# Queries of one batch item transposed by DMA instead of TensorE, with the loads behind them held and reordered

## The chip, the cores and the metric

One core of a Trainium2 chip runs the whole kernel. The metric is the device time of one execution in microseconds; a median of several runs is given. Before the change it is 173.47 us (172.95 to 173.8, 4 runs). A kernel counts as faster or slower when it differs by more than 2%.

## The reference, cut to what matters

Four batch items with 8 heads, 768 positions and head width 64 pass through block-sorted attention, and the result through a small MLP.

```python
P = sinkhorn(sort_net)                           # 5 rounds, 8x8 blocks per head
k_sorted = einsum('bhij,bhjcd->bhicd', P, k_b)   # also for v
scores = scale * matmul(q_b, k_sorted^T)         # per block of 96 positions
attn = softmax(scores)
x = matmul(attn, v_sorted)                       # then heads side by side
out = maximum(x @ w1, x @ w2) @ w_out            # for every position
```

## The kernel before

The program is laid out by hand: each engine executes its own list in the order of the Python code. The MLP of item b runs beside the attention of item b+1, as "units" of matmuls with "steps" of attention between them. An eviction copies a result from PSUM, where matmuls write, to SBUF; a transfer lands when its data are in place. "Packing" sets the queries of two heads side by side, and "turning" copies reorder loaded values. The parts that matter here:

```python
def pair_q(b, two):            # VectorE (DVE) packs two heads' queries side by side
    nc.vector.tensor_copy(out=q_pair[b][...], in_=q_raw[b][...])

def q_transposes(b, half):
    if b > 1:                  # items 2 and 3: transposed by DMA, from the sync queue
        nc.sync.dma_start_transpose(out=qT[b][...], in_=q_pair[b][...])
        return
    ps = ps_bf16("tq_ps")      # items 0 and 1: on TensorE (PE); for item 1, 12 matmuls per half
    ...
    evac(qT[b][...], ps, ...)  # and an eviction from PSUM

def load_rest():               # called after an early unit of item 0
    load_q(1)
    load_k(2)
...
9: [pair_q(1, 0), pair_q(1, 1), load_v(2), load_v(3), load_q(2)],   # after unit 9
...
# the copies that turn the values of items 2 and 3 follow values steps of item 1:
tns = [lambda c=c: turn(both, c) for c in range(0, BLK, 12)]
VA[1:6] = [(lambda f=f, g=g: (f(), g())) for f, g in zip(VA[1:6], tns)]
TR[0:2] = [(lambda f=f, g=g: (f(), g())) for f, g in zip(TR[0:2], tns[5:])]
```

PSUM is one pool of four buffers (`psum = tc.tile_pool(name="psum", bufs=4, ...)`), and every matmul group needs one. Loads are issued by GpSimd (POOL), and cast float32 to bfloat16 on the way.

The softmax here doesn't subtract the row's maximum and nothing guards it: scores larger than these inputs give would overflow.

Of the kernel before, what the change touches and what calls it, by code (L numbers as in the profile page):

```python
# [9 lines left out]

FP32 = mybir.dt.float32
BF16 = mybir.dt.bfloat16
TWICE = 1


@with_exitstack
def kernel(
# [16 lines left out]
    nc = tc.nc  # L34
# [12 lines left out]
    R = S // 128  # L47
    PB = 128 // NB
    HP = H // 2
# [5 lines left out]
    const = ctx.enter_context(tc.tile_pool(name="const", bufs=1))  # L55
# [13 lines left out]
    def ps_bf16(name):  # L69
        return psum.tile([128, 2048], BF16, tag="ps", name=name)  # L70
# [28 lines left out]
    def evac(out_ap, in_ap, n, two_x=False, eng=None):  # L99
        a_ns, d_ns = (200 + n) / 1.2, (130 + (n / 2 if two_x else n)) / 0.96  # L100
        if eng:
            load[eng] += a_ns if eng == "A" else d_ns
        if (eng or pick(a_ns, d_ns)) == "A":
            nc.scalar.copy(out=out_ap, in_=in_ap)  # L104
        else:
            nc.vector.tensor_copy(out=out_ap, in_=in_ap)  # L106
# [5 lines left out]
    q_raw, qT = {}, {}  # L112
# [15 lines left out]
    def load_q(b):  # L128
        t = qpool.tile([128, H, R * D], BF16, tag="q_raw", name="q_raw", bufs=1)
        nc.gpsimd.dma_start(out=t, in_=q[b].rearrange("h (p r) d -> p h (r d)", r=R))  # L130
        q_raw[b] = t
# [9 lines left out]
    def load_k(b):  # L141
        k_raw[b] = kpool.tile([128, HB * D], BF16, tag="k_raw", name="k_raw")
        n = HB * D // NCH
        for ci in range(NCH):
            nc.gpsimd.dma_start(  # L145
                out=k_raw[b][:, ci * n : (ci + 1) * n],
                in_=k_src[b, :, ci * n : (ci + 1) * n],
            )

    def load_v(b, c0=0, pieces=2):  # L150
        r0 = (b % 2) * 64
        n = (BLK - c0) * D // pieces
        for m in range(pieces):
            nc.gpsimd.dma_start(
                out=v_raw[r0 : r0 + 64, c0 * D + m * n : c0 * D + (m + 1) * n],
                in_=v_src[b, :, c0 * D + m * n : c0 * D + (m + 1) * n],
            )
# [19 lines left out]
    ident = const.tile([128, 128], BF16, tag="ident", name="ident")  # L177
# [26 lines left out]
    def turn_v(rows, eng, c0, c1, d0=0, d1=D):  # L204
        dst = v_dc[rows, 0 : D * BLK].rearrange("p (d c) -> p d c", c=BLK)[:, d0:d1, c0:c1]
        src = v_raw[rows].rearrange("p (c d) -> p d c", d=D)[:, d0:d1, c0:c1]
        for _ in range(TWICE):
            if eng == "A":
                nc.scalar.copy(out=dst, in_=src)
            else:  # L210
                nc.vector.tensor_copy(out=dst, in_=src)  # L211


    rowsum = const.tile([G, NB], FP32, tag="rowsum", name="rowsum")
# [107 lines left out]
    q_pair = {}  # L322
# [11 lines left out]
    def q_transposes(b, half, eng=None):  # L334

        if half == 0:
            qT[b] = qpool.tile([128, HP, R, 128], BF16, tag="qT", name="qT")
        if b > 1:
            nc.sync.dma_start_transpose(
                out=qT[b][:, half * 2 : half * 2 + 2].rearrange("p h r c -> p (h r) c"),  # L340
                in_=q_pair[b][:, half * 2 : half * 2 + 2].rearrange("p h r e -> p (h r e)"),
            )
            return
        ps = ps_bf16("tq_ps")
        for m in range(2 * R):
            hp, r = half * 2 + m // R, m % R
            c = slice(m * 128, (m + 1) * 128)
            if b in q_pair:
                nc.tensor.matmul(  # L349
                    ps[:, c], q_pair[b][:, hp, r], ident, is_transpose=True, start=True, stop=True  # L350
                )
                continue
            for h2 in range(2):
                nc.tensor.matmul(  # L354
                    ps[h2 * 64 : h2 * 64 + 64, c],
                    q_raw[b][:, hp + 4 * h2, r * D : (r + 1) * D],
                    ident,
                    is_transpose=True,
                    start=True,
                    stop=True,  # L360
                )
        evac(
            qT[b][:, half * 2 : half * 2 + 2].rearrange("p h r c -> p (h r c)"),
            ps[:, 0 : 2 * R * 128],
            2 * R * 128,
            two_x=True,
            eng=eng,
        )
# [275 lines left out]
    def att(b):  # L644

        SC = [lambda u=u: scores(b, u) for u in range(8)]
        VA = [lambda u=u: values(b, u) for u in range(8)]
        TR = [lambda t=t: x_transposes(b, t) for t in range(4)]
        return SC, VA, TR
# [20 lines left out]
    SC, VA, TR = att(0)  # L670
# [33 lines left out]
    def turn(rows, c0):  # L704
        turn_v(rows, "D", c0, c0 + 12)
        load["D"] += 800

    def load_rest():
        load_q(1)
        load_k(2)  # L710

    tail = {
        0: [VA[4]],
# [13 lines left out]
        9: [  # L727
            lambda: pair_q(1, 0),
            lambda: pair_q(1, 1),
            lambda: load_v(2),  # L730
            lambda: load_v(3),
            lambda: load_q(2),
        ],
        22: [lambda: block_diagonals(2)],
        23: [lambda: block_diagonals(3)],
# [8 lines left out]
    for b in range(B):  # L744
        units = [lambda t=t: moe_h(b, 0, t, None if b else "A") for t in range(4)]
        if b == 0:
            units[0] = lambda: None
            units[1] = lambda: None
        wps = [lambda dmt=dmt: w_product(dmt, "A" if dmt == 1 else None) for dmt in range(4)]
        if b == 0:  # L750
            units += wps[:2]
        units += [lambda t=t: moe_h(b, 1, t) for t in range(4)]
        cost = [1.3] * 8
        if b == 0:
            units += wps[2:]
            cost[4:4] = [1.7] * 2
            cost += [1.7] * 2
        units += [
            lambda ti=ti, part=part: moe_out(b, ti, part)
            for ti in range(6 if b < B - 1 else 4)  # L760
            for part in range(2)
        ]
        cost += [1.3] * 12
        if b == B - 1:
            units += [
                lambda: moe_out_last(4, [(0, 512, "D")]),
                lambda: moe_out_last(5, [(0, 256, "A"), (256, 384, "D"), (384, 512, "A")]),
            ]
        steps, lo = [], 2
        if b < B - 1:  # L770
            qs = [lambda half=half: q_transposes(1, half) for half in range(2)]
            if b < 2:
                tail[18 - 4 * b] = [lambda two=two: pair_q(b + 2, two) for two in range(2)]
                tail[18 - 4 * b] += [lambda half=half: q_transposes(b + 2, half) for half in range(2)]
            ks = [lambda t=t, b=b: sort_k(b + 1, t) for t in range(3)]
            SC, VA, TR = att(b + 1)

            def group(*fs):
                return [lambda: [f() for f in fs]]

            if b == 0:
                lo = 10
                tail[9][2:2] = ks
                vs = [lambda t=t: sort_v(1, t) for t in range(4)]
                tns = [lambda c=c: turn(both, c) for c in range(0, BLK, 12)]
                VA[1:6] = [(lambda f=f, g=g: (f(), g())) for f, g in zip(VA[1:6], tns)]
                TR[0:2] = [(lambda f=f, g=g: (f(), g())) for f, g in zip(TR[0:2], tns[5:])]
                SC[7:] = [lambda f=SC[7], g=tns[7]: (f(), g())]
                steps = group(*vs[:3]) + qs[:1] + group(*SC[0:2], vs[3]) + qs[1:] + VA[:1]
                steps += group(*SC[2:5]) + VA[1:2]  # L790
            elif b == 1:
                vs = [lambda t=t: sort_v_pair(2, t) for t in range(8)]
                steps = group(*ks) + group(*SC[0:2], vs[0], late_loads)
                steps += group(*vs[1:4]) + group(*vs[4:7]) + group(*SC[2:4], vs[7]) + VA[:2]
            else:
                steps = group(*ks) + group(*SC[0:2])
                steps += VA[:1] + group(*SC[2:5]) + VA[1:2]
            rest = SC[4:] if b == 1 else SC[5:]
            steps[-1:] = group(VA[1], TR[0])
            steps += VA[2:3] + group(VA[3], TR[1])  # L800
            steps += group(*rest[:-1]) + VA[4:5] + rest[-1:] + group(VA[5], TR[2])
            steps += VA[6:7] + group(VA[7], TR[3])
        done = 0
        for n, unit in enumerate(units):
            unit()
            for step in tail.get(n, []):
                step()
            total = sum(cost[lo:-2])
            want = -(-len(steps) * sum(cost[lo : n + 1]) // total)
            while done < min(want, len(steps)):  # L810
                steps[done]()
                done += 1
        tail = {}
# [28 lines left out]
```

## Time and profile before

| | before |
|---|---|
| median time | 173.47 us |
| span of the profiled execution | 172.3 us |
| PE busy | 161.7 us, 94% |
| DVE busy | 88.4 us, 51% |
| item 1's MLP starts (PE) | 73.34 us |
| last loads of the first stage land | 58.9 us |

PE is the bound. The start of item 1's MLP is a good milestone: behind it both kernels do the same work on PE. Its line before the change:

```profile
73.34 4.07 PE L576 MATMUL h_ps<-xT,w_sb 128*128 128x384 bf16 x24
```

In the line of an instruction the columns are start, length, engine, source line, operation, output and input, count, and in brackets how long the engine was idle before it and what ended that.

### The profile page before, as it was taken

The page shows a single profiled execution, that of the slowest core. Times are in us where ns is not written, and L with a number is a line of the kernel's source. Part 1 is how long each engine was busy: PE and PEld are TensorE (multiplying, and loading weights), DVE is VectorE, ACT ScalarE, POOL GpSimd, SP SyncE. Part 2 cuts the span into 40 slices and gives each one's busy share as a digit, 9 for nine tenths or more (in the row PEclk, how much of TensorE's full clock was granted, in tenths as well). Part 3 has the DMA queues.
Part 4 walks back from the last instruction along what each step waited for, and adds up shares of the span by engine and source line. Part 5 has one row for each costly group of instructions (what it writes and reads, how often), then busy time and mean ns, then how long its engine had stood idle before and what let it go on. Part 6 is the DMA issues. An engine that isn't in the chain of part 4 may idle for free.

```text
span 172.3 us, 4531 instructions
## 1 busy us (share of the span) xinstructions
PE 161.7 (94%) x1997; PEld 98.1 (57%) x2015; DVE 88.4 (51%) x194; ACT 83.8 (49%) x101; POOL 24.5 (14%) x40
## 2 busy tenths in 40 slices
PE   7899999989999999998989899999999999999990
PEld 7847766735666555456655445575554546654470
DVE  5879677679656399810685255044452422320130
ACT  4599875864745554069971532465605404312000
POOL 7953362251300000000600000000000000000000
PEclk9999999999999999999999999999999999999998
DMA  3999999999999352993497549920035173000342
GB/s 49 201 206 207 199 207 210 207 205 207 220 212 199 60 167 51 166 233 122 58 203 117 101 135 203 182 109 4 0 51 147 37 198 125 0 0 0 122 183 65
DMA packets 29811, 23.11 MB, mean 134 GB/s; under 512 B 16672, under 2 KB 24736, under 8 KB 29792
## 3 DMA queue, kind: packets, MB, share of 16 engines
q0 software_dynamic: 10304, 12.58, 42.9%
q1 hardware_dynamic: 19200, 10.04, 23.2%
q8 instruction: 16, 0.26, 0.6%
q10 hardware_dynamic: 288, 0.20, 0.4%
q14 instruction: 3, 0.02, 0.0%
HBM read 25.17 MB, written 6.29 MB: 183 GB/s over the span
## 4 chain that ended last, share of the span: by engine, by line
PE 79%; DMA 7%; ACT 6%; POOL 2%; DVE 2%; issue 2%; ACTq 0%; POOLq 0%
PE out_ps L603 36%; PE h_ps L576 24%; DMA q_raw<-in_q_dram 7%; PE o_ps L473 5%; PE wc_ps L554 4%; PE s_ps L446 3%; PE k_ps L379 2%; ACT kT L104 2%; ACT g L590 1%; DVE g L592 1%; ACT w2T L104 1%; PE tw_ps L531 1%; PE tq_ps L349 1%; PE tq_ps L354 1%; POOL k_raw L145 1%
## 5 line engine op out<-in xcount | busy, mean ns | idle before, releaser
L603 PE MATMUL out_ps<-wo_sb,g 128*128 128x512 bf16 (+2 forms) x197 | 47.0, 362 | 1.1 <-ACT o L104 0.5
L576 PE MATMUL h_ps<-xT,w_sb 128*128 128x384 bf16 x256 | 44.8, 326 | 0.8 <-DVE g L592 0.6
L576 PEld LDWEIGHTS <-w_sb 128*128 128x128 bf16 x256 | 24.2, 97 | 16.3 <-issue 0.6
L454 ACT ACTIVATE e<-s_ps 96x768 bf16<-96x768 f32 x32 | 24.2, 807 | 15.8 <-PE s_ps L446 15.7
L603 PEld LDWEIGHTS <-g 128*128 128x128 bf16 x208 | 17.7, 97 | 15.9 <-issue 0.5
L590 ACT ACTIVATE g<-h_ps 128x768 bf16<-128x768 f32 x22 | 17.8, 813 | 16.4 <-PE h_ps L576 16.4
L104 ACT COPY o<-out_ps 128x1024 f32<-128x1024 f32 x10 | 10.1, 1012 | 31.4 <-PE out_ps L603 31.4
L603 PE MATMUL out_ps<-wc,xT 128*128 128x512 bf16 (+2 forms) x103 | 24.9, 362 | 0.1
L490 DVE TENSOR_TENSOR x<-o_ps,rs 96x512 bf16<-96x512 f32 x32 | 22.0, 687 | 1.1
L592 DVE TENSOR_SCALAR g<-h_ps 128x768 bf16<-128x768 f32 x10 | 9.6, 958 | 15.9 <-PE h_ps L576 15.6
L484 DVE RECIPROCAL rs<-o_ps 96x8 f32<-96x8 f32 x32 | 6.4, 201 | 21.7 <-PE o_ps L473 21.5
L603 PEld LDWEIGHTS <-xT 128*128 128x128 bf16 x104 | 9.9, 97 | 11.0
L211 DVE COPY v_dc<-v_raw 64x768 bf16<-64x768 bf16 (+2 forms) x18 | 15.5, 902 | 0.4 <-DMA v_raw<-in_v_dram 0.3
L473 PEld LDWEIGHTS <-e 96*128 96x128 bf16 x256 | 11.6, 97 | 6.6 <-DVE x L490 0.5
L106 DVE CAST v_sb<-v_ps 96x1024 bf16<-96x1024 f32 x7 | 8.5, 1215 | 11.8 <-PE v_ps L421 8.4
L473 PE MATMUL o_ps<-v_sb,e 96*128 96x65 bf16 x256 | 13.1, 193 | 0.1
L104 ACT CAST v_sb<-v_ps 96x1024 bf16<-96x1024 f32 x9 | 8.7, 1014 | 2.0 <-PE v_ps L400 1.9
L446 PEld LDWEIGHTS <-kT 64*128 64x128 bf16 x256 | 6.0, 94 | 6.2 <-issue 4.2
L446 PE MATMUL s_ps<-qT,kT 64*128 64x96 bf16 x256 | 8.7, 204 | 0.7 <-ACT kT L104 0.6
L104 ACT CAST kT<-k_ps 128x1024 bf16<-128x1024 f32 x9 | 8.6, 1021 | 0.7 <-PE k_ps L379 0.7
L82 PEld LDWEIGHTS <-fill 128*128 128x128 bf16 x109 | 7.6, 128 | 2.2 <-DVE fill L73 1.2
L554 PE MATMUL wc_ps<-wo_sb,w2T 128*128 128x512 bf16 x29 | 7.4, 380 | 0.7 <-ACT w2T L104 0.5
(76 smaller groups left out, 130.0 us busy)
## 6 DMA issues: line engine op xcount, KB each, us to landing
out_dram<-o SPq DMA_DIRECT2D x11, 512.0 KB, 3.0
k_raw<-in_k_dram POOLq DMA_DIRECT2D x12, 256.0 KB, 10.4
q_raw<-in_q_dram POOLq DMA_DIRECT2D x4, 768.0 KB, 12.6
v_raw<-in_v_dram POOLq DMA_DIRECT2D x6, 384.0 KB, 13.6
w_sb<-in_moe_w_dram POOLq DMA_DIRECT2D x3, 512.0 KB, 15.9
wo_sb<-in_moe_w_out_dram POOLq DMA_DIRECT2D x2, 512.0 KB, 19.4
v_raw<-in_v_dram POOLq DMA_DIRECT2D x3, 256.0 KB, 4.9
w_sb<-in_moe_w_dram POOLq DMA_DIRECT2D x2, 256.0 KB, 14.3
```

The costliest lines, as they stand in the source:

```text
L104: nc.scalar.copy(out=out_ap, in_=in_ap)
L106: nc.vector.tensor_copy(out=out_ap, in_=in_ap)
L211: nc.vector.tensor_copy(out=dst, in_=src)
L446: nc.tensor.matmul(ps[:, h2 * 512 + ii * 128 : h2 * 512 + ii * 128 + BLK], kT[b][rows, (hp * 8 + i) * BLK : (hp * 8 + i) * BLK + 128], rhs ...
L454: nc.scalar.activation(out=e[:, 0 : 8 * BLK].rearrange("p (t c r) -> p t c r", t=8, r=R), in_=ps[0:BLK].rearrange("p (t f) -> p t f", t=8) ...
L473: nc.tensor.matmul(ps[:, h2 * 512 + ii * 65 : h2 * 512 + (ii + 1) * 65], e[:, (h2 * 4 + ii) * BLK : (h2 * 4 + ii) * BLK + 128], v_sb[:, m0 ...
L490: nc.vector.tensor_tensor(out=x, in0=ov[:, :, :, 0:D], in1=rs.to_broadcast([BLK, 2, 4, D]), op=ALU.mult,)
L554: nc.tensor.matmul(wc_ps[0][:, m * 512 : (m + 1) * 512], w2T[:, fb, dmt * 128 : (dmt + 1) * 128], wo_sb[:, fb, :], start=(fb == 0), stop=( ...
L576: nc.tensor.matmul(h_ps[t][:, m * 512 : m * 512 + TCH], w1_sb[:, hp, fb * 128 : (fb + 1) * 128], xT[:, b % 2, ch, hp % 2, hp // 2, :], sta ...
L590: nc.scalar.activation(out=g, in_=src, func=AF.Relu)
L592: nc.vector.tensor_scalar(out=g, in0=src, scalar1=0.0, scalar2=None, op0=ALU.max)
L603: nc.tensor.matmul(dst, g_tiles[b, ch, m // 2][:, m % 2, off : off + 128] if m < NFB else xT[:, b % 2, ch, hp % 2, hp // 2, off : off + 12 ...
```

## The change

The intent: take the 24 transposes of item 1's queries off PE, the busy engine, by handing them to the DMA engines, as is done for items 2 and 3. While they run no load is to disturb them, so all later loads wait for them, by way of a one-element copy on GpSimd that reads the transposed result. Behind it the loads leave as values, keys, queries. (A loop over `TWICE = 1` and the branch for item 1's PE transposes also go, and the sorting of item 1's keys is put behind the new issues.)

```diff
-        if b > 1:
+        if b > 0:
             nc.sync.dma_start_transpose(
...
     def load_rest():
         load_q(1)
+
+    def middle_loads():
+
+        held = const.tile([1, 1], BF16, tag="held_m", name="held")
+        nc.gpsimd.tensor_copy(out=held, in_=qT[1][0:1, HP - 1, R - 1, 0:1])
+        load_v(2)
+        load_v(3)
         load_k(2)
+        load_q(2)
...
             lambda: pair_q(1, 0),
             lambda: pair_q(1, 1),
-            lambda: load_v(2),
-            lambda: load_v(3),
-            lambda: load_q(2),
+            lambda: q_transposes(1, 0),
+            lambda: q_transposes(1, 1),
+            middle_loads,
...
-                steps = group(*vs[:3]) + qs[:1] + group(*SC[0:2], vs[3]) + qs[1:] + VA[:1]
+                steps = group(*vs[:3]) + group(*SC[0:2], vs[3]) + VA[:1]
```

More of the change, by code (lines that the diff above doesn't have):

```diff
@@ L12 @@
 BF16 = mybir.dt.bfloat16
-TWICE = 1
 @with_exitstack
@@ L206, in turn_v @@
         src = v_raw[rows].rearrange("p (c d) -> p d c", d=D)[:, d0:d1, c0:c1]
-        for _ in range(TWICE):
-            if eng == "A":
-                nc.scalar.copy(out=dst, in_=src)
-            else:
-                nc.vector.tensor_copy(out=dst, in_=src)
+        if eng == "A":
+            nc.scalar.copy(out=dst, in_=src)
+        else:
+            nc.vector.tensor_copy(out=dst, in_=src)
     rowsum = const.tile([G, NB], FP32, tag="rowsum", name="rowsum")
@@ L347, in q_transposes @@
             c = slice(m * 128, (m + 1) * 128)
-            if b in q_pair:
-                nc.tensor.matmul(
-                    ps[:, c], q_pair[b][:, hp, r], ident, is_transpose=True, start=True, stop=True
-                )
-                continue
             for h2 in range(2):
@@ L770 @@
         if b < B - 1:
-            qs = [lambda half=half: q_transposes(1, half) for half in range(2)]
             if b < 2:
@@ L782 @@
                 lo = 10
-                tail[9][2:2] = ks
+                tail[9][4:4] = ks
                 vs = [lambda t=t: sort_v(1, t) for t in range(4)]
```

## The prediction

> **What bounds the kernel now.** I read the page first, then the chain of work that ended last, then the instructions of DVE, GpSimd's queue and the sync queue in order of time between 27 and 76 us, and the busy time in stretches of 4 us. The page says who is the bound, and how the transfers lie in time:
>
> ```profile
> PE 161.7 (94%) x1997; PEld 98.1 (57%) x2015; DVE 88.4 (51%) x194; ACT 83.8 (49%) x101; POOL 24.5 (14%) x40
> ...
> DMA  3999999999999352993497549920035173000342
> GB/s 49 201 206 207 199 207 210 207 205 207 220 212 199 60 167 51 166 233 122 58 203 117 101 135 203 182 109 4 0 51 147 37 198 125 0 0 0 122 183 65
> ```
>
> TensorE (PE) is at 94%, so the time falls only by what leaves PE or what it waits for, and every wait put into its path costs in full. The DMA row (slices of 4.3 us) is full from the start to about 56 us at a steady 205 GB/s: the loads run back to back.
>
> The stage that the change touches, item 1's attention beside item 0's MLP, in stretches (columns: stretch, length, busy us of each engine, clock, DMA share, GB/s):
>
> ```profile
> 44.00:48.00 4.00, 3.95 (x124) 2.83 (x125) 2.24 (x3) 2.63 (x3) 1.58 (x2) 1.00 1.12 219
> 48.00:52.00 4.00, 3.79 (x70) 2.67 (x68) 2.18 (x2) 2.19 (x3) 0.00 (x0) 1.00 1.03 213
> 52.00:56.00 4.00, 3.76 (x54) 2.59 (x50) 2.79 (x4) 2.17 (x3) 0.00 (x0) 1.00 1.18 197
> 56.00:60.00 4.00, 3.94 (x49) 2.08 (x49) 1.33 (x4) 2.20 (x3) 0.00 (x0) 1.00 0.41 64
> 60.00:64.00 4.00, 4.00 (x53) 2.23 (x53) 3.93 (x8) 2.52 (x3) 0.00 (x0) 1.00 0.62 180
> 64.00:68.00 4.00, 3.94 (x35) 1.88 (x33) 3.97 (x8) 1.68 (x2) 0.00 (x0) 1.00 0.26 51
> ```
>
> DVE (third busy column) is half idle until 60 us, and then full: 3.93 and 3.97 of 4.00 us. So here, against its 51% overall, DVE has no slack. What fills it, in order of time (start, length):
>
> ```profile
> 59.06 0.69 DVE L490 TENSOR_TENSOR x<-o_ps,rs 96x512 bf16<-96x512 f32 x1
> 59.66 1.57 DVE L211 COPY v_dc<-v_raw 128x768 bf16<-128x768 bf16 x2
> 61.15 0.21 DVE L484 RECIPROCAL rs<-o_ps 96x8 f32<-96x8 f32 x1
> ...
> 66.62 1.02 DVE L328 COPY q_pair<-q_raw 128x1536 bf16<-128x1536 bf16 x2
> ```
>
> The 59.66 copies turn the values of items 2 and 3; the 66.62 pair packs the queries of item 2. Both read what the loads bring, and neither waits today: the values' issues at 37.16 to 43.97 us land between 49.6 and 55.1 (12.4, 12.8, 14.0 and 11.1 us to landing), the queries issued at 45.31 land at 58.9.
>
> The chain over the removed work (start, us, what):
>
> ```profile
> 48.10 1.02 ACT v_sb L104
> 49.12 0.04 issue
> 49.16 0.83 PE tq_ps L349 x12
> ...
> 51.76 1.02 ACT wc L104
> 52.78 0.04 issue
> 52.82 0.83 PE tq_ps L349 x12
> ```
>
> Both groups of 12 transposes are on the path, each just after the eviction of an older PSUM buffer. That shows how the four buffers are handed out: the second group took the one that the wc eviction freed, although others had been given back; the oldest released in program order comes next. I use that below.
>
> **What the Trainium skill says.** "DMA: Bandwidth & Descriptors", section "Queues, rings and completion order": each DMA engine serves the queues it has work for in turn, by packet. So transposes from the sync queue and loads from GpSimd share the same engines: holding the loads keeps the transposes short, but later transposes and stores will slow the held loads. No row above measures that sharing alone. "VectorE: DVE Perf Modes", section "The three transpose paths": a DMA transpose is slower in itself than TensorE's (1309 against 390 ns for 128x128) but lands in SBUF without PSUM. Here the 12 on PE took 0.83 us, and a DMA one of the same half 3.8 to 4.4 us to landing. "PSUM — Partial Sum Buffer", section "Engine vs sequencer instructions": the queues of VectorE, ScalarE and GpSimd are strict FIFO. The trace agrees, as far as DVE's order above is the program's: a DVE copy that waits for a load holds up the evictions behind it.
>
> **The change, part by part.** Removed from PE: 24 transposes in two groups of 0.83 us, 1.66 us, all on the path. Also gone are about 0.35 us of PE waits for the buffers they needed. From DVE: two evictions of qT of 0.95 us, which ran while DVE had slack: worth nothing directly. Two PSUM turns fewer. The packing of item 1's queries (1.03 us of DVE from 43.99) stays.
>
> Added: two DMA transposes. The packing ends at 45.02, the sync queue is empty then (its first transpose today is at 59.77), so the first goes out at 45.1. From item 2's pair (67.73: the first instruction takes 2.58 us and lands after 4.4, the second lands after 3.8) and item 3's (101.57: 1.67 us, second lands after 4.2) the halves land at about 49.3 and 51.0 to 51.5. PE reaches the first scores at 49.1 to 49.2, as fewer steps stand before them: a wait of some 0.2 us. The half for heads 2 and 3 is wanted only after 53 us. Net so far: 1.66 + 0.35 - 0.2, about 1.8 us gained; I take 1.7. With nothing else, item 1's MLP (73.41 today) would start at 71.7.
>
> Moved: values 2 and 3, keys 2 and queries 2 leave after a GpSimd copy that reads qT. The same construction for item 3 took 0.5 us from the copy (82.46) to the first issue (82.95). So the first load goes out at about 51.7, instead of keys at 29.95 and values at 37.16. Queries 1 land at 44.0 as before (27.68 + 16.3), since they stood in front of the moved loads anyway. Hence the DMA engines, full today until about 57, do nothing but two transposes from 44 to about 53 us: 9 us of load time lost.
>
> When do values land? Keys and queries of item 3 are the same 1.57 MB from an empty queue: issued from 82.95, the last landed at 94.3 (84.53 + 9.8), 11.35 us. So the last piece of the values lands at 51.7 + 11.35 = 63.1, with some sharing with one transpose and one store 63.2 (my estimate). DVE wants it (its second turning copy, channels 60 to 71) at about 57.3, since the steps are now 13 instead of 15 and item 1's second values step comes one unit earlier than today. DVE stands still for nearly 6 us.
>
> What PE does meanwhile: it goes on through two output units and two values steps to the third, then wants a buffer for the scores of step 5. Following the buffers by the rule above, that one is the buffer of values step 2, whose eviction stands behind the waiting copy. PE arrives at about 60.7; the eviction ends at 63.2 + 0.8 (copy) + 0.9 (reciprocal and multiply) = 64.9. Wait: 4.2 us.
>
> Then the queries of item 2: after the values another 1.57 MB (keys, queries), at 205 GB/s 7.7 us, plus about 1.6 us for a store and a transpose among them: 63.1 + 7.7 + 1.6 = 72.4. Today DVE needs 6.2 us from the second turning copy (60.44) to the packing (66.62), full throughout. So it arrives at 63.2 + 6.2 = 69.4 and waits 3 us more. From the packing to item 1's last values eviction it needs 5.0 us (66.62 to 71.65): 77.4. That eviction frees the buffer of the next MLP unit, by the same rule. So item 1's MLP starts at about 77.4 instead of 73.41: 4.0 us late. From there all is PE work as before, and nothing in the stages after it makes up for a late start.
>
> Sum: 173.4 + 4.0 = 177.4. If the sharing with stores costs nothing, queries land near 70.8, the second wait is 1.4 us, and PE's own work (71.7 + 4.2 = 75.9) sets the start: +2.5, 175.9. I put 177.0.
>
> **Rivals.** (1) The gain stands: PE loses 1.8 us of work and no wait takes its place, 171.6. For it: keys and values are put in the order of need, and PE has three other buffers to run on. Against it: the values' arrival at about 63 us against a need at 57, and a DVE without slack from 60 on; at least 3 of these 4 us must show on PE. (2) Only the first wait counts: queries come before DVE asks for them, because DVE is late itself. Then +2.5 at most, 175.9, and within 2%. (3) The transposes are slow, or the loads slower than those of item 3, as they run beside two item-1 transposes and two stores: each us of delay goes through both waits to the end, 178 to 180. (4) PE has matmuls whose clock falls in the waits; today the clock is 1.00 in every stretch above, and waits of 4 us would have to be punished for that to matter. I give it no number.
>
> **Range and chances.** The mean of the cases is 177.0. Below it lies an earlier release (51.2) with loads at full rate, about 174.5; above it rival 3, 179.2. The line of 2% slower is 176.9, nearly my middle: slower 0.53, same 0.42, faster 0.05 (that needs 3.5 us, twice what is removed).
>
> **What would show it.** Right: no transposes of packed queries on PE; DMA share near zero between 45 and 53; GpSimd's held copy at 51 to 52; DVE idle before a turning copy of the values for 4 to 6 us, released by the values' load; PE idle some 4 us before scores of item 1; a second DVE wait before the packing of item 2; item 1's first MLP matmuls at 75.5 to 78. Wrong: values landing before 60 us, or PE running through the DVE wait because the scores got another buffer. Then the time is near 171.6 and my buffer step or my load step has failed.

## The result, and the profile after

The changed kernel takes 180.58 us (180.26 to 180.8, 4 runs) against 173.47 us. The ratio is 1.0411, with a 95% interval of 1.038 to 1.0442: slower. Ratios are the mean time of one kernel's fast runs over that of the other's of the same rounds, so they are not quite the ratio of the medians.

The page of the changed kernel: engine totals, and the DMA engines in 40 slices of 4.5 us.

```profile
PE 162.7 (91%) x1991; PEld 97.2 (55%) x1991; DVE 87.5 (49%) x193; ACT 82.9 (47%) x100; POOL 24.3 (14%) x41
...
DMA  4999999996938999889379545940022353200333
GB/s 54 204 205 207 199 207 215 196 202 97 120 60 156 191 199 219 153 198 176 134 107 204 90 133 138 247 147 7 2 44 47 118 162 89 77 0 0 118 118 118
```

The row of loads that was full to 56 us now has a hole from the tenth to the twelfth slice (97, 120 and 60 GB/s), and the loads end near 75 us instead. The busy time of PE has not fallen by 1.66 us but risen by 1.0: part of the work ran at a lower clock. (A few matmul records are also missing from the page before, 197 of 208 in one group.)

Of the stretches shown in the prediction those that changed most, and one more (busy us of PE, weight loads, DVE, ACT, POOL; then clock, DMA share, GB/s):

```profile
44.00:48.00 4.00, 4.00 (x127) 2.83 (x122) 2.25 (x3) 2.59 (x4) 0.00 (x0) 1.00 0.37 85
48.00:52.00 4.00, 1.76 (x51) 1.64 (x47) 1.22 (x1) 2.20 (x3) 0.00 (x0) 0.87 1.06 116
52.00:56.00 4.00, 4.00 (x33) 2.08 (x31) 1.81 (x2) 1.14 (x2) 3.39 (x8) 0.71 0.48 71
...
64.00:68.00 4.00, 2.16 (x31) 1.31 (x32) 3.79 (x7) 1.50 (x2) 0.00 (x0) 1.00 1.17 195
...
76.00:80.00 4.00, 2.13 (x12) 0.94 (x13) 3.83 (x11) 1.01 (x1) 0.00 (x0) 1.00 0.90 205
```

Before, PE was busy all but 0.24 us at most of each of those stretches. Now it stands still for about 2 us in three of them: from 48, from 64 and from 76. The DMA engines are not idle all the time that the loads are held: with the two transposes, and the first loads at the end, their share is 0.37, 1.06 and 0.48 in the three stretches from 44.

GpSimd's queue and DVE, in order of time:

```profile
52.26 0.18 POOL L707 COPY held<-qT 1x1 bf16<-1x1 bf16 x1 [23.65 <-DMA qT<-q_pair]
52.78 2.08 POOL L153 DMA_DIRECT2D v_raw<-in_v_dram  x4 [0.34 <-ACT e L447]
...
56.44 0.96 POOL L129 DMA_DIRECT2D q_raw<-in_q_dram  x1
```

```profile
61.85 0.83 DVE L209 COPY v_dc<-v_raw 128x768 bf16<-128x768 bf16 x1 [1.38 <-DMA v_raw<-in_v_dram]
64.14 0.81 DVE L209 COPY v_dc<-v_raw 128x768 bf16<-128x768 bf16 x1 [1.47 <-DMA v_raw<-in_v_dram]
...
74.59 1.03 DVE L326 COPY q_pair<-q_raw 128x1536 bf16<-128x1536 bf16 x2 [4.18 <-DMA q_raw<-in_q_dram]
```

The copy that holds the loads runs at 52.26, when the second transposed half has landed. DVE then waits three times for what those loads bring; before, it waited for none of them. And PE, whose first wait ends with the transpose, and each later one with an eviction that stood behind a waiting DVE copy:

```profile
51.03 0.82 PE L439 MATMUL s_ps<-qT,kT 64*128 64x96 bf16 x16 [2.24 <-DMA qT<-q_pair]
...
65.84 0.51 PE L439 MATMUL s_ps<-qT,kT 64*128 64x96 bf16 x16 [1.96 <-DVE x L483]
...
77.23 0.20 PE L286 MATMUL pe<-p_bf,sel_k 32*128 32x64 bf16 x1 [1.63 <-DVE x L483]
...
79.63 4.07 PE L569 MATMUL h_ps<-xT,w_sb 128*128 128x384 bf16 x24 [0.64 <-DVE x L483]
```

The last line is item 1's MLP: 79.63 instead of 73.34, 6.3 us late. From there to the end it is 98.6 us, and it was 99.0 us before. So the whole loss within the span is made before 79.63. The chain of work that ended last says by what (start, us, what):

```profile
45.49 5.50 DMA qT<-q_pair
...
56.44 18.13 DMA q_raw<-in_q_dram
74.56 0.02 issue
74.59 1.03 DVE q_pair L326 x2
...
79.63 4.09 PE h_ps L569 x24
```

Before, 79% of the chain was PE. Here it runs over the first transpose, the release of the loads, 18.1 us from the issue of item 2's queries to their landing, and DVE. (For the release the profile names the exponential behind the first scores, which ended at 52.46. The held copy ended at 52.44, and no load reads that exponential, so I take the copy to be what released them; in e2, e3 and e4 the chain goes through it.) PE's waits and its slow clock between 52 and 74 us are not on it.

### The profile page after: what moved, and what is told of

The parts are those of the page before. It is cut to its first block, busy times and chain, and to the rows that moved or that the text cites. A ratio compares the mean times of both kernels' runs of the same rounds, so it can differ in the third digit from the quotient of the medians.

```text
span 178.2 us, 4504 instructions
## 1 busy us (share of the span) xinstructions
PE 162.7 (91%) x1991; PEld 97.2 (55%) x1991; DVE 87.5 (49%) x193; ACT 82.9 (47%) x100; POOL 24.3 (14%) x41
## 4 chain that ended last, share of the span: by engine, by line
PE 58%; DMA 14%; DVE 12%; issue 7%; ACT 6%; POOL 2%; DVEq 0%; ACTq 0%
PE out_ps L596 24%; PE h_ps L569 20%; DMA q_raw<-in_q_dram 10%; DMA qT<-q_pair 3%; PE k_ps L372 3%; PE o_ps L466 2%; DVE x L483 2%; DVE g L585 2%; PE wc_ps L547 2%; PE s_ps L439 2%; ACT kT L103 1%; PE v_ps L393 1%; POOL v_raw L153 1%; ACT w2T L103 1%; PE tw_ps L524 1%
## 5 line engine op out<-in xcount | busy, mean ns | idle before, releaser
L596 PE MATMUL out_ps<-wo_sb,g 128*128 128x512 bf16 (+2 forms) x208 | 48.3, 363 | 0.5 <-ACT o L103 0.5
L103 ACT COPY o<-out_ps 128x1024 f32<-128x1024 f32 x9 | 9.1, 1012 | 36.4 <-PE out_ps L596 29.5
L583 ACT ACTIVATE g<-h_ps 128x768 bf16<-128x768 f32 x21 | 17.0, 812 | 15.3 <-PE h_ps L569 15.3
L585 DVE TENSOR_SCALAR g<-h_ps 128x768 bf16<-128x768 f32 x11 | 10.5, 956 | 24.7 <-PE h_ps L569 24.6
L103 ACT CAST v_sb<-v_ps 96x1024 bf16<-96x1024 f32 x10 | 9.7, 1034 | 1.9 <-PE v_ps L393 1.4
L103 ACT CAST kT<-k_ps 128x1024 bf16<-128x1024 f32 x10 | 9.5, 1022 | 0.5 <-PE k_ps L372 0.5
L105 DVE CAST v_sb<-v_ps 96x1024 bf16<-96x1024 f32 x6 | 7.3, 1211 | 4.8 <-PE v_ps L393 4.8
L547 PE MATMUL wc_ps<-wo_sb,w2T 128*128 128x512 bf16 x32 | 8.6, 411 | 0.5 <-ACT w2T L103 0.5
```

The source lines that it names most:

```text
L103: nc.scalar.copy(out=out_ap, in_=in_ap)
L547: nc.tensor.matmul(wc_ps[0][:, m * 512 : (m + 1) * 512], w2T[:, fb, dmt * 128 : (dmt + 1) * 128], wo_sb[:, fb, :], start=(fb == 0), stop=( ...
L583: nc.scalar.activation(out=g, in_=src, func=AF.Relu)
L585: nc.vector.tensor_scalar(out=g, in0=src, scalar1=0.0, scalar2=None, op0=ALU.max)
L596: nc.tensor.matmul(dst, g_tiles[b, ch, m // 2][:, m % 2, off : off + 128] if m < NFB else xT[:, b % 2, ch, hp % 2, hp // 2, off : off + 12 ...
```

## The experiments

The theory to test: the lateness of the held loads, read early in DVE's queue, sets the start of item 1's MLP (A). Its rivals: the DMA transposes themselves, with PE's wait for them and the slow clock after it, make the loss (B); or the hold was needless. "Before" in these rounds had medians from 173.44 to 173.67 us.

### e1 and e5: the change without the hold

```diff
-        held = const.tile([1, 1], BF16, tag="held_m", name="held")
-        nc.gpsimd.tensor_copy(out=held, in_=qT[1][0:1, HP - 1, R - 1, 0:1])
```

> The changed kernel without the hold: values, keys and queries leave as soon as their buffers allow, so the two transposes of item 1's queries run beside loads. Theory A (the lateness of the held loads is the whole loss, but the hold has a reason): no DVE wait before the turning copies or the packing of item 2, but the transposes land 8 to 10 us after their issue at 45.5, as the two item-1 transposes beside loads did in the changed kernel (10.2 and 8.3 us), so PE waits for the first scores until 53.5 to 55.5, 4.5 to 6.5 us, the clock falls, and the time is 177 to 180. Rival B (the hold is needless; transposes land in 4 to 5.5 us anyway): PE waits 1 to 2 us and the time is 172 to 174.

> The kernel without the hold once more, for a profile: the first one's profiled run was an outlier of 904 us. Its timed runs took 186.3 to 187.2 us, 13.4 us more than before, where theory A of the first submission said 3.5 to 6.5 more. Theory A': transposes beside loads are held up far more than the 8 to 10 us I assumed, the first half lands 14 to 18 us after its issue, PE waits for it 11 to 14 us, and neither turning copies nor packing wait for loads. Rival: the transposes land within 10 us and the time is lost later, at a DVE wait for loads that the transposes slow in turn.

e1 measured 187.04 us median, ratio 1.0763 (1.0729 to 1.0797). Its profiled execution was an outlier of 904 us, which is not used: all of PE ran several times slower in it, and the cause is not known. e5, one look at the same kernel, took 187.28 us in a run whose state is unknown, and agrees with e1's fast runs. In e5, the first score step on PE, and the time from issue to landing (last number) of the first half's transpose:

```profile
62.12 0.82 PE L439 MATMUL s_ps<-qT,kT 64*128 64x96 bf16 x16 [13.23 <-DMA qT<-q_pair]
```

```profile
qT<-q_pair SPq DMA_TRANSPOSE x1, 16.6
```

Beside the loads the transpose took 16.6 us to land instead of 5.5, and PE waited 13.23 us for it. No DVE wait for loads followed. So the direction of theory A was right in e1 and its size wrong; theory A' of e5, made when e1's time was known, holds in all its numbers. The hold has its reason: without it the kernel is 13.4 us slower than before, with it 7.1.

### e2: the hold alone, transposes left on PE

```diff
     def load_rest():
         load_q(1)
-        load_k(2)
+    def middle_loads():          # held copy, then v2, v3, k2, q2, as in the change
...
...             # load_v(2), load_v(3) and load_q(2) leave the list of unit 9
-                ... + qs[1:] + VA[:1]
+                ... + group(qs[1], middle_loads) + VA[:1]
```

> The kernel before, transposes on PE as they were, with only the hold and the new order of loads; the hold ends with the eviction of the second transposed half, at about 54.8. Theory A (the lateness of the loads sets the end): first load at 55.4, last piece of values 11.4 us later at 66.8, queries 21.8 us later at 77.2, item 1's MLP 5.0 us after that at 82.2 instead of 73.4, time 181 to 183.5: slower than the changed kernel, with no DMA transpose of item 1's queries. Rival B (the DMA transposes themselves, with PE's wait for them and the fall of the clock, are the loss): 173 to 175.

185.55 us, ratio 1.0694 (1.0648 to 1.074). There is no DMA transpose of item 1's queries in it, and it is slower than the change, as its held copy ran later (54.68 instead of 52.26). DVE's wait before the packing, and the start of item 1's MLP:

```profile
78.00 1.03 DVE L328 COPY q_pair<-q_raw 128x1536 bf16<-128x1536 bf16 x2 [5.31 <-DMA q_raw<-in_q_dram]
```

```profile
83.70 5.49 PE L576 MATMUL h_ps<-xT,w_sb 128*128 128x384 bf16 x24
```

Rival B falls: the hold and the new order of the loads make a loss by themselves. The landing came 0.8 us later than expected and the MLP start 1.5 us later; the 24 matmuls then took 5.49 us instead of 4.07, at half clock after a PE wait of 4.47 us, which I had not counted. Together these put the time above the range.

### e3: queries 2 before keys 2

```diff
         load_v(3)
-        load_k(2)
         load_q(2)
+        load_k(2)
```

> The changed kernel with queries 2 loaded before keys 2. Theory A (the landing of queries 2 at 74.6 sets the start of item 1's MLP at 79.6): they land at 69.5 to 70.5, when DVE comes to the packing (70.4), its second wait of 4.2 us goes, the MLP starts at 76.8 to 77.6 as PE's own work allows, and the time falls by 2 to 2.8 us to 177.8 to 178.6. Keys at 74.6 are wanted only after 80. Rival B (PE's waits and the slow clock before 66 us set the end): 180 to 180.8 as before.

179.51 us, ratio 1.0359 (1.0316 to 1.0402) against 1.0411 for the change: about 0.9 us less, where 2 to 2.8 was expected. DVE's wait before the packing was gone in the profile, as A said, but the MLP started at 78.41, not at 77.2. PE had a longer wait for the scores of step 5:

```profile
65.42 0.54 PE L439 MATMUL s_ps<-qT,kT 64*128 64x96 bf16 x16 [4.52 <-DVE x L483]
```

The mean clock was 0.72 in the stretch from 64 to 68 and 0.85 in the next. From here to the MLP the chain stays on PE, and from these scores to the next it took 5.00 us where the change needed 3.39. So with that DVE wait gone, the DVE waits for the values and the slow clock, some 1.6 us, are the path. The intervals of e3 and the change overlap; the profile is the better witness here.

### e4: dummy matmuls in PE's first wait

```diff
-group(*SC[0:2], vs[3])
+group(lambda: scores(1, 0, 4608), SC[1], vs[3])     # 9 x 512 columns of zeros first
```

> The changed kernel with nine dummy matmuls of 512 columns (about 2 us) on PE before the first scores of item 1, so that PE is busy while it waits for the transpose. Theory A (first wait and slow clock are hidden, since the loads set the end): the clock stays at 1.00 from 51 to 55, PE comes to the scores of step 5 some 1 to 1.5 us sooner and waits that much longer there, and the time stays within 0.5 us of the changed kernel, 180.1 to 181. Rival B (the slow clock costs its 1.5 us in the end): 179 to 179.4.

180.71 us, ratio 1.0403 (1.0344 to 1.0462): the same as the change. The stretch from 52 us, and the scores of step 5:

```profile
52.00:56.00 4.00, 3.91 (x42) 1.92 (x39) 3.18 (x4) 1.22 (x3) 3.28 (x7) 1.00 0.43 61
```

```profile
65.82 0.51 PE L439 MATMUL s_ps<-qT,kT 64*128 64x96 bf16 x16 [3.33 <-DVE x L483]
```

The clock stayed at 1.00 where it was 0.71, PE came to step 5 earlier, waited 3.33 instead of 1.96 us, and went on at 65.82 instead of 65.84. PE's first wait and the slow clock were hidden behind the loads. Two things limit this. In e4's profile the first transpose had landed after 3.7 us, so there was hardly a wait left to fill; and behind the longer second wait the clock fell (0.66 in the stretch from 68 us), which was hidden as well, since DVE still waited for the queries until 74.92.

### e8: dummy matmuls in PE's second wait, on top of e3

```diff
+            if b == 0:
+                SC[5] = lambda: scores(1, 5, 9216)
```

> e3 (queries before keys) with 18 dummy matmuls of 512 columns, about 4 us, before the scores of step 5, where PE waited 4.5 us in e3 and its clock then was at a half from about 65.5 to 69. Theory A (with the second DVE wait gone the slow clock is on the path): the clock stays at 1.00, item 1's MLP starts 1 to 1.8 us sooner than e3's 78.4, time 177.7 to 178.7. Rival B (something else sets e3's MLP start): 179.2 to 179.8 as e3.

183.97 us, ratio 1.0597 (1.0554 to 1.0641): 4.5 us slower than e3, so neither theory. The experiment was badly made. The dummy matmuls write the buffer of the score step, and that buffer was what PE waited for. DVE and PE in it:

```profile
64.10 0.69 DVE L483 TENSOR_TENSOR x<-o_ps,rs 96x512 bf16<-96x512 f32 x1
```

```profile
64.84 7.00 PE L81 MATMUL s_ps<-fill 128*128 128x512 bf16 x18 [3.95 <-DVE x L483]
```

They began at 64.84, just behind the eviction of values step 2 (64.10 + 0.69), and then cost 7.0 us at half clock. So this run does not test whether the slow clock is what e3 lost; for that there is only e3's own chain. But it does show the step of the buffers: matmuls that read nothing but zeros waited for that eviction, so the PSUM buffer was what was missing.

### e6 and e7: the readers moved behind the loads

e6 is e3 with the turning copies, item 2's packing and the transposes behind it placed later; e7 moves the first score steps as well.

```diff
-                VA[1:6] = [(lambda f=f, g=g: (f(), g())) for f, g in zip(VA[1:6], tns)]
-                TR[0:2] = ...; SC[7:] = ...
+                tail[18] = tns[0:2]; tail[19] = tns[2:3]; tail[20] = tns[3:4]; tail[21] = tns[4:5]
+                tail[22] = tail[22] + [pair_q(2, 0), pair_q(2, 1), q_transposes(2, 0), q_transposes(2, 1)]
...             # in item 1's units: tail[0] = tns[5:7]; tail[1] = tns[7:8]
# e7 also:
-                steps = group(*vs[:3]) + group(*SC[0:2], vs[3]) + VA[:1]
+                steps = group(*vs[:3]) + group(vs[3]) + group(*SC[0:2]) + VA[:1]
```

> Hold and DMA transposes as in the change, queries before keys as in e3, and the eight turning copies and item 2's packing moved behind the last output units of item 0 and into item 1's first two MLP units, when their loads have landed. Theory A (the held loads cost time only because DVE's queue stands behind their early readers): DVE no longer waits before 62 us, PE does not wait for the scores of step 5, item 1's MLP starts at 71.5 to 73.5 as the first transposes land early or late, and the time is 171.5 to 174: all of the loss is gone, with at most the 1.7 us of the removed transposes gained. Rival B (hold and DMA transposes cost in other ways too, such as slow transposes and stores beside the held loads, which item 1's MLP waits for): 176 or more.

> As e6, with the first two score steps of item 1 behind the fourth values sort and the wc product, some 2.3 us later on PE, so that the first transpose has landed when it comes. Theory A: where e6 loses up to 2.2 us and a slow clock at the first scores, this one does not; time 171.5 to 172.5, spread between runs smaller than e6's. If the transposes land early in all of e6's runs, both are the same within 0.4 us.

e6: 177.52 us, ratio 1.0226 (1.02 to 1.0252). e7: 177.86 us, ratio 1.0203 (1.0159 to 1.0247), two of its six runs slow. Against the change more than 3 us of the loss went, but not all: rival B of e6 was right. DVE waited for no load, PE reached item 1's MLP at 72.20, and then stood still. In e6, the second part of the MLP's first matmuls, and the time to landing of the two transposes that it needs:

```profile
75.54 5.41 PE L569 MATMUL h_ps<-xT,w_sb 128*128 128x384 bf16 x22 [2.84 <-DMA xT<-x]
```

```profile
xT<-x SPq DMA_TRANSPOSE x1, 10.1
...
xT<-x SPq DMA_TRANSPOSE x1, 14.6
```

The transposes of item 1's attention output now ran beside the held loads. They took 10.1 and 14.6 us; before, on quiet engines, 2.9 and 2.8. PE waited 2.84 us and ran at a clock of 0.57 afterwards. e7 gained nothing over e6 and missed its range; in e6's profile the first scores had not waited for the transpose.

### e9, e10 and e11: those two transposes back on PE

```diff
-        if b > 0:
+        if b > 1 or (b == 1 and t > 1):
             nc.sync.dma_start_transpose(out=xT[...], ...)
# e9 on e6, e10 on e7; e11 is e9 with each of the two one step later:
-            steps[-1:] = group(VA[1], TR[0])
-            steps += VA[2:3] + group(VA[3], TR[1]) + group(*rest[:-1])
+            steps += group(VA[2], TR[0]) + VA[3:4] + group(*rest[:-1], TR[1])
```

> e6 with item 1's first two x transposes on PE again (16 matmuls, two evictions) instead of by DMA beside the held loads, where they landed only 10.1 and 14.6 us after their issue and item 1's MLP waited for them from 72.7 to 75.5, then ran at half clock. Theory A (transposes beside loads are what is left of the loss in e6): that wait and the slow clock go, 0.7 us of PE work comes back, item 1's MLP starts at 72.8 to 73.6, time 172.5 to 174.2, within 0.6% of before. Rival B (another wait stands behind that one): 175.5 or more.

> e7 with the same: as e9, with the first two score steps 2.3 us later on PE. Theory A: 172.5 to 174.2 too; below e9 by up to 1 us if e9's first scores wait for the transpose in some runs. If either is below the kernel before by more than its interval, it is the version that beats both.

> e9 with its two x transposes one step later on PE, behind the next values step and the scores of step 6. In e9 each stood right behind the values step that feeds it, so PE waited 1.02 us for DVE twice. Theory A (nothing else of the loss is left): the two waits go, item 1's MLP starts at 73.2 to 73.7 instead of 75.4, time 173.0 to 174.0, the same as before within 0.4%: with the hold paid for in full by later readers, the change is worth its 1.7 us less the 1.2 us of PE time and evictions for the two x transposes. Rival B (the hold still costs): 174.5 or more.

e9: 175.36 us, ratio 1.0104 (1.0082 to 1.0125). e10: 176.34 us, ratio 1.0184 (1.0154 to 1.0214), unclear. Both miss their ranges. In e9 the wait for the DMA was gone, but I had put each transpose right behind the values step that feeds it, and PE waited 1.02 us for DVE twice; in e10 it was 1.02 and 1.90 us. e11 mends that: 172.81 us, ratio 0.9979 (0.9957 to 1.0002). Item 1's MLP in it:

```profile
72.85 4.07 PE L569 MATMUL h_ps<-xT,w_sb 128*128 128x384 bf16 x24
```

It started 0.5 us earlier than before the change, with the hold and the two DMA transposes still in place; that and the time lie a little below the ranges that I gave (73.2 us and 173.0 us). Between the change and e11 lie the order of the loads (e3), the later readers (e6) and two transposes back on PE (e9, e11). So the loss is accounted for: held loads read early by DVE, and transposes beside the loads behind that. e11 may beat the kernel before by 0.2%, but its interval reaches 1.0002; it counts as the same.

## Why the prediction was right or wrong

The direction and the path were right: held loads, DVE copies that wait for them, and item 1's MLP behind DVE. For the direction I had given only 0.53. The step that failed is the time line of the held loads, in two terms: when they are released (51.7 predicted, 52.78 measured) and what they lose by sharing the DMA engines (1.6 us predicted, 2.7 left over in the measurement). With these, item 1's MLP starts at 79.63 instead of 77.4. I said 177.0, somewhat under my own sum of 177.4, with 179.2 as the upper case, and it is 180.58.

| step | predicted | measured |
|---|---|---|
| transposes gone from PE | 24 | 24 |
| first half lands | 49.3 | 50.98 |
| PE's wait for it | 0.2 us | 2.24 us |
| first held load issued | 51.7 | 52.78 |
| last piece of the values lands | 63.2 | about 64.1 |
| DVE comes to the second turning copy | 57.3 | 62.7 |
| DVE's wait there | nearly 6 us | 1.47 us, and 1.38 us before the first copy |
| PE's wait before the scores of step 5 | 4.2 us | 1.96 us |
| PE goes on there | 64.9 | 65.84 |
| queries 2 land | 72.4 | 74.57 |
| DVE's wait for them | 3.0 us | 4.18 us |
| item 1's MLP starts | 77.4 | 79.63 |

**The milestone.** The MLP start is 2.2 us later than in the sum, and two terms make it. "So the first load goes out at about 51.7" was 1.1 us early: the packing ended about 0.4 us later in this run, and the second transpose, for which the hold waits, took 5.2 us to land (4.9 to 5.3 in e3, e4, e6, e7, e9 and e11), where those of items 2 and 3 had taken 3.8 to 4.4. And "about 1.6 us for a store and a transpose among them" was too small: from the first load to the queries' landing it took 21.8 us, of which 11.35 + 7.7 = 19.05 are the loads as I counted them, so 2.7 us are left for the sharing, with two transposes and a store. The kept traces support that: with the same make-up it took 22.0 us in e4 and 22.8 us in e2, but about 20.4 us in e9 and e10, where two stores and, until the last 2.5 us, no transpose ran beside the loads. The 1.57 MB of values by themselves came as worked out from item 3's loads: 64.1 - 52.78 = 11.3 us against 11.35.

**The waits on PE.** I left the transpose's wait at 0.2 us, and gave the slow clock no number. Both occurred: 2.24 us, then a clock of 0.5. They explain why the waits on DVE and before step 5 were shorter than predicted: PE came later, and DVE behind it. In e3, where the first scores did not wait for the transpose, these waits had about the size predicted: 4.55 and 0.88 us on DVE, 4.52 us on PE. In the change they cost nothing beyond that, as e4 shows; in e3 the slow clock is on the path. Waits on PE before a point that a load decides must not be added up.

**The buffers.** The rule for handing out PSUM buffers, read from two lines of the kernel before, held: the scores of step 5 waited for the eviction of values step 2 (e8), and the MLP's first unit for the last values eviction (the 0.64 us wait at 79.63).

**The rivals.** Rival 1 (the gain stands) and 2 (only the first wait counts) were wrong. Rival 3, slow transposes and slow loads, is what came on top, and I had put it at 178 to 180 and taken 179.2 from it as the upper case. Rival 4, the clock, got no number; the change did not need one, but e2 and e3 did.

**The signs.** Four that I named for being right did not come: the DMA share was not near zero between 45 and 53 us (it was zero only outside the transposes, and 1.06 on average from 48 to 52), DVE's waits for the values were not 4 to 6 us, PE's wait before step 5 was not 4 us, and the MLP started after 78. The held copy came just outside 51 to 52, at 52.26.

**What my account lacked.** I reasoned that sharing slows the held loads, and did not ask what the loads do to the transposes behind them. In the changed kernel that is hidden, but in e6 it is what is left of the loss.

**Open.** The milestone accounts for 6.3 us, the medians differ by 7.1. The profiled span of the kernel before was itself at the long end (172.3, against 171.0 to 172.2 in its timed runs). Outside the span the changed kernel spends 2.4 to 2.5 us (180.69 - 178.2) where the kernel before spends about 1.9 (173.67 - 171.8); why, no run shows. Also open is why the first transpose of item 1's queries landed after 5.5 us in the change's profile, with no load beside it, where e3, e4, e6, e7, e9 and e11 show 3.6 to 3.7 us; and why the second took longer than those of items 2 and 3.

## What to carry to other kernels

Before holding loads to make room for something, add up how long no load will move, and compare that with the slack of each load's first reader, above all where the reader stands in an in-order queue in front of work that frees buffers. Here about 9 us without loads met some 5 us of slack (values landed at 55.1 and were read from 59.66). In this kernel DMA transposes and bulk loads belong in different stretches of time: where the loads could not leave (e6), TensorE was the cheaper place for the transpose (e11).

## What the Trainium skill lacked or had wrong

- "DMA: Bandwidth & Descriptors" says in "Rules for kernel authors" of a transpose next to ordinary DMAs that it "needs nothing". That is about correct results, and all runs here were correct. For the time a number is missing: a transpose of queries or of attention output landed after 2.7 to 5.5 us with no load beside it, and after 6.5 to 16.6 us beside loads from GpSimd (the change, e5, e6).
- "TensorE: Matmul & The Clock Gate" gives in "HAM oscillation — how this bites in real kernels" the rule "no PE-idle gaps >~3.4µs". Here shorter gaps were enough: behind an idle time of 2.24 us the clock was halved (the lines below, of the changed kernel). After 2.84 us (e6) and 1.90 us (e2, from 69.5 us) it fell too. After gaps of 1.96 and 1.63 us in the changed kernel it did not, so the length of a gap alone does not decide. The traces show a grid. Each fall between 40 and 95 us lasted 3.41 us or a multiple of it (3.41 in the changed kernel, 6.83 in e8, 13.65 in e5). Counted from a run's first fall in steps of 3.41 us, the step just before each fall held 1.90 us or more of PE idle time (1.90 in e2, 2.15 in the changed kernel; the ends of matmuls are modelled); the gap of 1.96 us was split into 0.7 and 1.2 by the end of a step, and 1.63 us in one step is the most that left the clock alone.

```profile
50.00:51.00 1.00, 0.00 (x0) 0.00 (x0) 0.00 (x0) 0.00 (x0) 0.00 (x0) 0.97 0.35 70
51.00:52.00 1.00, 0.97 (x23) 0.97 (x24) 0.00 (x0) 0.36 (x1) 0.00 (x0) 0.50 0.87 195
...
54.00:55.00 1.00, 1.00 (x6) 0.37 (x5) 0.00 (x0) 0.00 (x0) 1.00 (x3) 0.82 1.07 117
```

- "VectorE: DVE Perf Modes", "The three transpose paths", compares the paths for one 128x128 block alone. For choosing one, no page has what decided here: 12 blocks by DMA took 3.3 to 5.5 us to landing with no load beside them and 10.9 and 16.6 us beside loads (e5), against 0.83 us on PE and 0.95 us of DVE for the eviction.
